# A fused attention and two feed-forward layers on one core: one bank pair used in halves, one conversion step less, other planned costs, and products of zeros in the first units

## The chip, the cores and the metric

The kernel runs on one core of a Trainium2 chip. The metric is device microseconds of one execution. The kernel before was run three times: median 749.57 us, from 743.37 to 752.7. One further execution was profiled; it took 745.85 us and its span, from the first to the last instruction, is 744.1 us.

## The reference, cut to what matters

```
scores = scale * q @ k.T ; causal mask ; a = softmax(scores) ; local = a @ v
q_p = phi(q)                                  # max(x, 0) + min(exp(x), 1)
mem_out = (q_p @ M_prev) / (q_p @ z_prev + 1e-6)
x = g * mem_out + (1 - g) * local             # g = sigmoid(beta), B=2 H=8 S=576 D=64
g1 = elu(x @ w_in) ; x = g1 @ w_out           # 1152 tokens, 512 -> 2048 -> 512
out = sum over 4 experts of p_e * (relu(x @ w1[e]) @ w2[e])   # 512 -> 1024 -> 512
```

All inputs are float32. The weights of the first feed-forward layer reach the kernel as 64-bit floats.

## The kernel before, in words

The work runs in two parts. In the first part the tokens are in two groups: 384 tokens (0 to 191 of both batches) and 768 tokens (the rest). Attention is cut into units, each a pair of heads: four units F0 to F3 for the first group (both batches at once), then eight units R00 to R13 for the second group. While the R units run, the first group goes through the first feed-forward layer (tiles ua, da; class Moe1) and the second one (ub, db; Moe2). The second part does both layers for the second group with a scheme of seven products for eight.

The order of the instructions is written by a planner (class Plan). Each step names its engine, a cost in us, a rank, the steps that it comes after, and the buffers that it takes and gives back. The planner keeps a clock for each engine and always starts the step with the lowest rank that can start at that time by those costs. So the costs (act_cost, dve_cost, pool_cost and the figures in the calls of add) set only the order on each engine; on the chip an engine runs its instructions in that order and waits on semaphores.

A unit does these steps: load, load_v (SyncE); split_h (ACT) and split_l (POOL, for F0 DVE) cut q and k into a high and a low part; phi_r, phi_e, phi_p (ACT) make phi(q); mem (PE, line 1226) multiplies phi(q) with the memory into a PSUM region om, and mem_a, mem_i, mem_f (DVE, 1202, 1240, 1208) divide it into tm; score (PE, 1273), lowest (DVE, 1287), exp (ACT, 1296), trans (PE, 1332), evac (1337 DVE, 1339 ACT), values (PE, 1346 and 1355) make the local part in a PSUM region ov, and sum_a, sum_i, sum_f (DVE) divide it into tv; both (POOL, 1386) adds tm to tv; turn (PE, 1392) transposes it, and join_h, join_l split it into xh and xl. Both regions om and ov lie in one tile o of two banks, of which there is one: SLOTS has "o": 1, mem takes it and sum_f gives it back, so the planner puts the next unit's mem behind this unit's sum_f.

Each of the 16 weight tiles that come as 64-bit floats is loaded in two halves of 512 KB (line 206), converted half by half, split into wh (ACT, 239) and wl (POOL, 243), and stored as 32-bit floats for the second part (keep, 235). A half's conversion is upper (ACT, 215), which scales the upper words into a bank, then on DVE shift (219), lower (223) and sign (229). All but the first tile wait in the plan for F3's last score (GATE). Each half has two buffers, given back by sign.

keep_busy puts products of zeros (line 297, one bank wide) ahead of a PE step for which the planner's clock showed a wait of over 0.3 us, until 140 us of that clock. Sixteen such products stand at the start.

Of the kernel before, what the change touches and what calls it, by code (L numbers as in the profile page):

```python
# [59 lines left out]
def tile_kernel(  # L60
# [53 lines left out]

    def plan_small(plan, rank):
# [12 lines left out]
        plan.add(("gate_e",), "act", 0.2, rank, gate_e, [("load_gate",)])  # L128
        plan.add(("gates",), "dve", 0.3, rank, gates, [("gate_e",)])
        plan.add(("probs",), "dve", 1.0, 30.0, setup_probs)  # L130

    def setup_probs():
        nc.sync.dma_start(out=pr, in_=probs)
# [19 lines left out]
    SLOTS = {  # L153
        "raw": 2, "rv": 2, "qh": 2, "ql": 2, "pe": 1, "pp": 2, "pt": 2, "nm": 4, "nr": 4, "tm": 1, "tv": 1,
        "ph": 4, "s0": 1, "s1": 1, "t": 1, "o": 1, "m": 3,
        "wr": 3, "w64_0": 2, "w64_1": 2, "w": NW, "h": 5, "ev": 3,
# [8 lines left out]
    }  # L165

    GATE = ("F3", "score20")
    UNIT1 = 5.0
# [14 lines left out]
    def plan_weights(plan, i, rank):  # L183
# [26 lines left out]
        def upper(half):  # L210
            if half == 0:
                block()
            _, high = t[half]
            t["cv", half] = abank("m" if i < W_EARLY else f"s{half}", f"cv{i}_{half}")
            nc.scalar.activation(out=t["cv", half], in_=high.bitcast(F32), func=AF.Copy, scale=2.0 ** -112)

# [4 lines left out]
        def lower(half):  # L221
            c, low = t["cv", half].bitcast(I32), t[half][0]
            nc.vector.scalar_tensor_tensor(  # L223
                out=c, in0=low, scalar=29, in1=c, op0=ALU.logical_shift_right, op1=ALU.bitwise_or
            )

        def sign(half):
            high, wi = t[half][1], t["wr"][:, 512 * half:512 * half + 512].bitcast(I32)
            nc.vector.scalar_tensor_tensor(
                out=wi, in0=high, scalar=-(2 ** 31), in1=t["cv", half].bitcast(I32),  # L230
                op0=ALU.bitwise_and, op1=ALU.bitwise_or,
            )
# [13 lines left out]
        if k < NW1 and not second:  # L246
            ends = []
            for half in range(2):
# [8 lines left out]
                add(f"shift{half}", "dve", dve_cost(512), lambda half=half: shift(half))  # L257
                add(f"lower{half}", "dve", dve_cost(512), lambda half=half: lower(half))
                ends.append(("w", i, f"sign{half}"))
                plan.add(  # L260
                    ends[-1], "dve", dve_cost(512), rank, lambda half=half: sign(half), [last[0]], [],
                    [f"w64_{half}", ("m", ("w", i, f"upper{half}")) if bank == "m" else bank],
# [25 lines left out]
    def attention_pools(stack):  # L288
# [4 lines left out]
        for name in ("s", "t", "o"):  # L293
            at[name] = pool("ps_" + name, bufs=1, space=PSUM)

    def nothing(ps):
        nc.tensor.matmul(
            ps.rearrange("p (n k) -> p n k", k=P), zeros, zeros.unsqueeze(1).to_broadcast([P, ps.shape[1] // P, P]),
            start=True, stop=True,
        )  # L300

    waits = [0]

    def keep_busy(ps):

        for _ in range(waits[0]):
            nothing(ps)
        waits[0] = 0
# [708 lines left out]
    def act_cost(n, psum=False):  # L1017
        return 0.833e-3 * n + (0.052 if psum else 0.093)

    def dve_cost(n, fast=False):  # L1020
        return (0.521e-3 if fast else 1.042e-3) * n + 0.069

    def pool_cost(n):
        return 2.1e-3 * n + 0.15

# [98 lines left out]
    def plan_unit(plan, kind, b, c, start, spare, slack):  # L1124
# [65 lines left out]
        if kind == "F":  # L1190
            add("phi_p", "act", act_cost(nq), phi_p, ["phi_e", "split_l"], gives=["raw"])
        else:
            add("phi_p", "pool", 2.5e-3 * nq + 0.2, phi_p, ["phi_e"])
            add("phi", "pool", pool_cost(nq), phi, ["phi_p", "split_l"], gives=["raw", "pe"])
# [11 lines left out]
        def times(ps, name, out):  # L1206
# [3 lines left out]
            )  # L1210

        def mem():
            o = at["o"].tile([P, 2, 512], F32, tag="o", name=f"o{uid}")
            keep_busy(o[:, 0])
            o = o[:, :, :2 * nt * DV].rearrange(
                "p a (w t d) -> p w a t d", w=2, d=DV
            )
            unit["om"], unit["ov"] = o[:, 0], o[:, 1]
            for t in range(nt):
                for bi, r0, r in parts_of(t):  # L1220
                    q = qcol[t] + 2 * r0
                    for odd in (0, 1):
                        rows = slice(D * odd, D * odd + D)
                        terms = ("e", "phi") if kind == "F" else ("phi",)
                        for x in terms:
                            nc.tensor.matmul(
                                unit["om"][r0:r0 + r, odd, t], unit[x][rows, q:q + r],
                                unit["rv"][rows, MEMORY[kind] + bi], start=x == terms[0], stop=x == terms[-1],
                            )

        def mem_f():
            unit["tm"] = atile([P, 3, 2, D], F32, tag="tm", name=f"tm{uid}")[:, :nt]
            times(unit["om"], "nm_", unit["tm"])

        if kind == "F":
            add("mem", "pe", 0.15 * 2 * nt, mem, ["phi_p", "load_v"], ["o"], ["pp", "pe"])
        else:
            add("mem", "pe", 0.15 * nt, mem, ["phi", "load_v"], ["o"], ["pp"])
        add("mem_a", "dve", 0.12, lambda: quotient(unit["om"], 1e-6, wmem, "nm_"), ["mem", ("gates",)], ["nr"])
        add("mem_i", "dve", 0.1, lambda: nc.vector.reciprocal(out=unit["nm_"], in_=unit["nm_"]), ["mem_a"])  # L1240
        add("mem_f", "dve", dve_cost(NQ), mem_f, ["mem_i"], ["tm"], ["nr"])


# [9 lines left out]
        def score(t, n):  # L1253
# [6 lines left out]
            for odd in (0, 1):  # L1260
                tag = "m" if "m" in s_from[t, n] else f"s{odd}"
                unit["s", odd, t, n] = abank(tag, f"s{uid}{odd}{t}{n}")
            keep_busy(unit["s", 0, t, n])
            for bi, r0, r in parts_of(t):
# [28 lines left out]
        def expo(odd, t):  # L1293
            k = 2 * t + len(segments(tiles[t][1])) - 1
            blk = row(odd, t)
            nc.scalar.activation(out=blk, in_=blk, func=AF.Exp, scale=-1.0, bias=unit["nm"][odd][:, k:k + 1])  # L1296

        for t, n, a, z_ in pieces:
            first, last = (t, n) == pieces[0][:2], (t, n) == pieces[-1][:2]
            add(  # L1300
                f"score{t}{n}", "pe", 3 * (z_ - a) / 2400 + 0.2, lambda t=t, n=n: score(t, n),
                ["split_l"] + ["score{}{}".format(*pieces[0])] * (not first), s_from[t, n] + ["pt", "nm", "nm"] * first, ["qh", "ql"] * last,
# [57 lines left out]
        for g, blks in enumerate(groups):  # L1360
            col, final = P * len(blks), g == len(groups) - 1
            add(
                f"trans{g}", "pe", 0.109 * len(blks), lambda g=g: transposes(g),
                sorted({f"exp{t}{odd}" for t, o, _ in blks for odd in ((0, 1) if o == 2 else (o,))})
# [8 lines left out]
            add(  # L1373
                f"values{g}", "pe", 0.115 * len(blks), lambda g=g: values(g),
                ["mem", f"evac{g}"] + [f"values{g - 1}"] * (g > 0), [], ["ph"] + ["rv", "nm", "nm"] * final,
            )
# [8 lines left out]
        def both():  # L1385
            nc.gpsimd.tensor_tensor(out=unit["tv"], in0=unit["tv"], in1=unit["tm"], op=ALU.add)

# [35 lines left out]
    with ExitStack() as first, tc.manual_schedule():  # L1423
# [8 lines left out]
        plan.awake, plan.last = IDLE_END, 0.43 * WARM - 0.5  # L1432
        plan_small(plan, OFFSET["load"] + 3.0)
        for c in range(H // 2):
# [107 lines left out]
```

## Time and profile before

| what | value |
|---|---|
| median of three runs | 749.57 us (743.37 to 752.7) |
| profiled execution | 745.85 us, span 744.1 us |
| PE busy | 729.4 us, 98% |
| DVE, ACT, POOL busy | 409.0, 355.4, 422.2 us |
| DMA, mean over the span | 108 GB/s |

PE is TensorE's matmul row, PEld its weight loads, SP the engine that issues the transfers. A busy PE is no PE at its peak: products of zeros and products at half the clock count as busy too. PEclk is the granted TensorE clock as a share of 2.4 GHz.

### The profile page before, as it was taken

Reading aid. Unit: us, or ns where it says so; the run is one execution under the profiler, and the core shown is the slowest. Engines: PE = TensorE matmul, PEld = TensorE weight load, DVE = VectorE, ACT = ScalarE, POOL = GpSimd, SP = SyncE. Lnnn points to the kernel's source line nnn. Section 1 sums busy time; section 2 is a strip of 40 time slices with the busy share of each in tenths; the row PEclk is TensorE's granted clock in tenths of the full one; section 3 lists DMA queues with packets and bytes.
Section 4 is the critical chain, followed back from the end, with each engine's and each line's share of the span. In section 5 each row is a group of like instructions: output and inputs, shape, how many; then the busy total and the mean of one; then the engine's idle time right before and its main releaser. Section 6 shows DMA issues by size and latency. Waiting matters only on the chain.

```text
span 744.1 us, 11247 instructions
## 1 busy us (share of the span) xinstructions
PE 729.4 (98%) x4339; PEld 651.2 (88%) x4339; DVE 409.0 (55%) x876; ACT 355.4 (48%) x609; POOL 422.2 (57%) x253
## 2 busy tenths in 40 slices
PE   8999989999999999999899999999999999999997
PEld 5688878898898898889799999998989989899896
DVE  3687897734524435423672774865636446364562
ACT  6648578665445444422585663753423224232230
POOL 4337676786365361436998747397666455664210
PEclk9989999999999999999999999999999999999999
DMA  7449698453332321313323231212303113031002
GB/s 237 127 138 351 227 300 297 153 164 124 101 112 80 106 86 50 102 43 110 100 62 109 85 102 41 64 51 85 92 26 111 57 57 96 22 110 57 1 0 85
DMA packets 23541, 80.38 MB, mean 108 GB/s; under 512 B 2880, under 2 KB 2880, under 8 KB 23488
## 3 DMA queue, kind: packets, MB, share of 16 engines
q1 hardware_dynamic: 23488, 79.66, 33.0%
q8 instruction: 34, 0.56, 0.3%
q14 instruction: 19, 0.16, 0.1%
HBM read 68.90 MB, written 10.75 MB: 107 GB/s over the span
## 4 chain that ended last, share of the span: by engine, by line
PE 86%; DVE 6%; ACT 3%; DMA 2%; POOL 2%; issue 1%; SPq 0%; DVEq 0%; ACTq 0%
PE db L273 9%; PE db L275 9%; PE db L274 9%; PE oR L1346 4%; PE da L275 4%; PE da L273 4%; PE da L274 4%; PE ub L273 3%; PE ub L275 3%; PE ub L274 3%; PE tR L1332 3%; PE sR L1273 2%; DVE cv L223 1%; DVE cv L219 1%; PE oR L1355 1%
## 5 line engine op out<-in xcount | busy, mean ns | idle before, releaser
L243 POOL TENSOR_TENSOR wl<-wr,wh 128x1024 fp32r<-128x1024 f32 x72 | 171.7, 2392 | 168.0 <-ACT wh L239 161.6
L239 ACT ACTIVATE wh<-wr 128x1024 fp32r<-128x1024 f32 x72 | 75.6, 1057 | 97.3 <-PE db L274 64.2
L273 PE MATMUL db<-wh,hb 128*128 128x512 f32 x288 | 115.1, 400 | 0.0
L275 PE MATMUL db<-wl,hb 128*128 128x512 f32 x288 | 112.8, 392 | 0.0
L274 PE MATMUL db<-wh,hb 128*128 128x512 f32 x288 | 112.6, 391 | 0.0
L987 DVE SCALAR_TENSOR_TENSOR acc<-db,pr,acc 128x512 f32<-128x512 f32 x42 | 31.5, 750 | 70.9 <-PE db L275 70.9
L275 PE MATMUL da<-ha,wh 128*128 128x384 f32 x192 | 65.9, 343 | 2.1 <-POOL ha L402 2.0
L273 PE MATMUL da<-ha,wh 128*128 128x384 f32 x192 | 66.4, 346 | 0.5 <-ACT ha L848 0.3
L274 PE MATMUL da<-ha,wl 128*128 128x384 f32 x192 | 65.2, 339 | 1.5 <-POOL wl L243 1.5
L273 PEld LDWEIGHTS db<-wh,hb 128*128 128x128 f32 x288 | 54.2, 188 | 11.9 <-issue 1.3
L275 PEld LDWEIGHTS db<-wl,hb 128*128 128x128 f32 x288 | 54.1, 188 | 11.7
L274 PEld LDWEIGHTS db<-wh,hb 128*128 128x128 f32 x288 | 54.2, 188 | 10.3
L502 DVE SCALAR_TENSOR_TENSOR hb<-ub,hb 128x384 fp32r<-128x384 f32 x32 | 17.7, 553 | 53.9 <-ACT hb L499 53.9
L273 PE MATMUL ub<-yh,wh 128*128 128x384 f32 x128 | 46.1, 360 | 0.0
L275 PE MATMUL ub<-yl,wh 128*128 128x384 f32 x128 | 43.1, 337 | 0.0
L274 PE MATMUL ub<-yh,wl 128*128 128x384 f32 x128 | 43.0, 336 | 0.0
L275 PEld LDWEIGHTS da<-ha,wh 128*128 128x128 f32 x192 | 36.6, 190 | 4.1 <-POOL ha L402 3.5
L273 PEld LDWEIGHTS da<-ha,wh 128*128 128x128 f32 x192 | 36.5, 190 | 2.1 <-issue 0.7
L274 PEld LDWEIGHTS da<-ha,wl 128*128 128x128 f32 x192 | 36.5, 190 | 2.1 <-POOL wl L243 2.1
L1296 ACT ACTIVATE ptR<-ptR,nmR 128x576 f32<-128x576 f32 (+2 forms) x48 | 30.3, 661 | 15.6 <-DVE nmR L1287 15.6
L1346 PE MATMUL oR<-rvR,pfR 128*128 128x65 f32 x288 | 37.5, 271 | 0.0
L1346 PEld LDWEIGHTS oR<-rvR,pfR 128*128 128x128 f32 x288 | 35.5, 192 | 1.0 <-issue 0.2
(883 smaller groups left out, 1869.2 us busy)
## 6 DMA issues: line engine op xcount, KB each, us to landing
wr<-in_w SPq DMA_DIRECT2D x64, 512.0 KB, 3.5
w<-in_w SPq DMA_DIRECT2D x32, 512.0 KB, 5.7
wscr<-wr SPq DMA_DIRECT2D x16, 512.0 KB, 6.7
wr<-wscr SPq DMA_DIRECT2D x16, 512.0 KB, 3.3
qkR<-in_qk_r SPq DMA_DIRECT2D x8, 480.0 KB, 5.8
rvR<-in_vm_r SPq DMA_DIRECT2D x8, 390.0 KB, 3.1
out<-acc SPq DMA_DIRECT2D x8, 256.0 KB, 2.0
qkF<-in_qk_f SPq DMA_DIRECT2D x4, 416.0 KB, 5.5
```

Of the source, the lines that this page charges most:

```text
L219: nc.vector.tensor_scalar(out=c, in0=c, scalar1=3, scalar2=None, op0=ALU.logical_shift_left)
L239: nc.scalar.activation(out=t["wh"], in_=t["wr"], func=AF.Copy)
L243: nc.gpsimd.tensor_tensor(out=wl, in0=t["wr"], in1=f32(t["wh"]), op=ALU.subtract)
L273: nc.tensor.matmul(out, ah, bh, start=first, stop=False)
L274: nc.tensor.matmul(out, al, bh, start=False, stop=False)
L275: nc.tensor.matmul(out, ah, bl, start=False, stop=last)
L502: nc.vector.scalar_tensor_tensor(out=t["h"][:, 1], in0=t["ps"], scalar=0.0, in1=f32(t["h"][:, 0]), op0=ALU.max, op1=ALU.subtract)
L987: nc.vector.scalar_tensor_tensor(out=acc, in0=t["ps"], scalar=p, in1=acc, op0=ALU.mult, op1=ALU.add)
L1273: nc.tensor.matmul(unit["s", odd, t, n][:, :w], unit[x][rows, q], unit[y][rows, ks[odd]], start=m == 0 and r0 == 0, stop=m == 2 and final,)
L1296: nc.scalar.activation(out=blk, in_=blk, func=AF.Exp, scale=-1.0, bias=unit["nm"][odd][:, k:k + 1])
L1332: nc.tensor.transpose(pst[:, P * n:P * n + P], src, ident)
L1346: nc.tensor.matmul(unit["ov"][:, odd, t], pf[:, col:col + P], unit["rv"][:, at_], start=j == 0, stop=False)
```

## The change

- The tile o becomes one tile sums, made once; om and ov are its left and right half (256 columns of each of the two banks) with a planner slot of their own ("om", "ov"). mem takes om, mem_f gives it back; the first values takes ov, sum_f gives it back. values no longer comes after mem. tm has two buffers.
- In F units phi_e and phi_p are added on POOL (step phi), as R units do, and mem multiplies the sum: one product for each pair of operands in place of two.
- F3 (hurried) leaves tm in PSUM and does its last addition on DVE in place of POOL.
- The conversion's sign step is gone: upper uses Prelu with a slope of 2^32 for negative words in place of Copy, and lower writes the result.
- F units put at least one product of zeros at the head of the first score and of each trans, and at least two of half the width at the head of mem and of the first values.
- The planned costs of ACT, DVE, POOL, score, mem, values and trans are other figures; the load of the probabilities is a step of its own with a later rank, and the gates have a later rank.
- The scratch for dynamic DMA is 1024 bytes.

```
-        "raw": 2, ... "tm": 1, "tv": 1,
-        "ph": 4, "s0": 1, "s1": 1, "t": 1, "o": 1, "m": 3,
+        "raw": 2, ... "tm": 2, "tv": 1,
+        "ph": 4, "s0": 1, "s1": 1, "t": 1, "om": 1, "ov": 1, "m": 3,
...
+    FEWEST = {"F": 1, "R": 0}
...
-        plan.add(("gate_e",), "act", 0.2, rank, gate_e, [("load_gate",)])
-        plan.add(("gates",), "dve", 0.3, rank, gates, [("gate_e",)])
-        plan.add(("probs",), "dve", 1.0, 30.0, setup_probs)
+        plan.add(("gate_e",), "act", 0.4, later, gate_e, [("load_gate",)])
+        plan.add(("gates",), "dve", 0.3, later, gates, [("gate_e",)])
+        plan.add(("load_probs",), "sync", 0.1, 20.0, load_probs)
+        plan.add(("probs",), "dve", 1.0, 30.0, setup_probs, [("load_probs",)])
...
-            nc.scalar.activation(out=t["cv", half], in_=high.bitcast(F32), func=AF.Copy, scale=2.0 ** -112)
+            nc.scalar.activation(
+                out=t["cv", half], in_=high.bitcast(F32), func=AF.Prelu, scale=2.0 ** -112, alpha=2.0 ** 32
+            )
...
         def lower(half):
-            c, low = t["cv", half].bitcast(I32), t[half][0]
+            low, wi = t[half][0], t["wr"][:, 512 * half:512 * half + 512].bitcast(I32)
             nc.vector.scalar_tensor_tensor(
-                out=c, in0=low, scalar=29, in1=c, op0=ALU.logical_shift_right, op1=ALU.bitwise_or
-            )
-
-        def sign(half):
-            high, wi = t[half][1], t["wr"][:, 512 * half:512 * half + 512].bitcast(I32)
-            nc.vector.scalar_tensor_tensor(
-                out=wi, in0=high, scalar=-(2 ** 31), in1=t["cv", half].bitcast(I32),
-                op0=ALU.bitwise_and, op1=ALU.bitwise_or,
+                out=wi, in0=low, scalar=29, in1=t["cv", half].bitcast(I32),
+                op0=ALU.logical_shift_right, op1=ALU.bitwise_or,
             )
...
+        at["sums"] = at["o"].tile([P, 2, 512], F32, tag="o", name="sums")
...
-    def keep_busy(ps):
+    def keep_busy(ps, least=0):
-        for _ in range(waits[0]):
+        for _ in range(max(waits[0], least)):
             nothing(ps)
...
     def act_cost(n, psum=False):
-        return 0.833e-3 * n + (0.052 if psum else 0.093)
-    def dve_cost(n, fast=False):
-        return (0.521e-3 if fast else 1.042e-3) * n + 0.069
+        return 0.833e-3 * n + (0.09 if psum else 0.13)
+    def dve_cost(n):
+        return 1.042e-3 * n + 0.115
     def pool_cost(n):
-        return 2.1e-3 * n + 0.15
+        return 2.1e-3 * n + 0.2
...
         if kind == "F":
             add("phi_p", "act", act_cost(nq), phi_p, ["phi_e", "split_l"], gives=["raw"])
+            add("phi", "pool", pool_cost(nq), phi, ["phi_p"], gives=["pe"])
...
+        def side(what):
+            keep_busy(at["sums"][:, 0, 256 * what:256 * what + 256], 2 * FEWEST[kind])
+            return at["sums"][:, :, 256 * what:256 * what + nt * DV].rearrange("p a (t d) -> p a t d", d=DV)
...
-                        terms = ("e", "phi") if kind == "F" else ("phi",)
-                        for x in terms:
-                            nc.tensor.matmul(
-                                unit["om"][r0:r0 + r, odd, t], unit[x][rows, q:q + r],
-                                unit["rv"][rows, MEMORY[kind] + bi], start=x == terms[0], stop=x == terms[-1],
-                            )
+                        nc.tensor.matmul(
+                            unit["om"][r0:r0 + r, odd, t], unit["phi"][rows, q:q + r],
+                            unit["rv"][rows, MEMORY[kind] + bi], start=True, stop=True,
+                        )
+        hurried = uid == f"F{H // 2 - 1}"
...
-        if kind == "F":
-            add("mem", "pe", 0.15 * 2 * nt, mem, ["phi_p", "load_v"], ["o"], ["pp", "pe"])
-        else:
-            add("mem", "pe", 0.15 * nt, mem, ["phi", "load_v"], ["o"], ["pp"])
+        mem_cost = 0.2 + 0.224 * sum(len(parts_of(t)) for t in range(nt))
+        add("mem", "pe", mem_cost, mem, ["phi", "load_v"], ["om"], ["pp"])
...
-            keep_busy(unit["s", 0, t, n])
+            keep_busy(unit["s", 0, t, n], FEWEST[kind] * (n == t == 0))
...
-            keep_busy(pst)
+            keep_busy(pst, FEWEST[kind])
...
         def values(g):
+            if g == 0:
+                unit["ov"] = side(1)
...
-                ["mem", f"evac{g}"] + [f"values{g - 1}"] * (g > 0), [], ["ph"] + ["rv", "nm", "nm"] * final,
+                [f"evac{g}", "load_v"] + [f"values{g - 1}"] * (g > 0), ["ov"] * (g == 0), ["ph"] + ["rv", "nm", "nm"] * final,
...
-        add("sum_f", "dve", dve_cost(NQ), sum_f, ["sum_i"], ["tv"], ["o", "nr"])
-        add("both", "pool", pool_cost(NQ), both, ["sum_f", "mem_f"], gives=["tm"])
+        add("sum_f", "dve", dve_cost(NQ), sum_f, ["sum_i"], ["tv"], ["ov", "nr"])
+        eng = ("dve", dve_cost(NQ)) if hurried else ("pool", pool_cost(NQ))
+        add("both", *eng, both, ["sum_f", "mem_f"], gives=["om" if hurried else "tm"])
```

## Rows read from the trace of the kernel before

**Rows 1.** The page: busy time, share of the span and instructions of each engine.

```profile
PE 729.4 (98%) x4339; PEld 651.2 (88%) x4339; DVE 409.0 (55%) x876; ACT 355.4 (48%) x609; POOL 422.2 (57%) x253
```

**Rows 2.** Windows by stage: start:end, length, busy us of each engine, clock, DMA share, GB/s.

```profile
6.40:48.20 41.80, 39.71 (x405) 29.50 (x405) 25.44 (x95) 24.86 (x54) 12.33 (x9) 0.92 0.47 151
...
56.70:66.20 9.50, 7.68 (x32) 6.13 (x32) 8.89 (x15) 7.15 (x14) 7.72 (x5) 0.83 0.98 329
66.20:126.00 59.80, 56.33 (x325) 50.71 (x324) 47.97 (x88) 42.98 (x76) 41.44 (x26) 1.00 0.85 300
...
140.00:300.00 160.00, 160.00 (x1083) 138.56 (x1082) 69.12 (x191) 76.42 (x121) 86.35 (x48) 1.00 0.34 110
300.00:400.00 100.00, 97.60 (x553) 87.07 (x553) 45.74 (x91) 49.29 (x85) 65.79 (x39) 0.98 0.29 92
```

**Rows 3.** Windows of the products of zeros alone (line 297), PE's busy time first.

```profile
6.40:48.20 41.80, 11.23 (x45) 0.92 0.47 151
...
56.70:66.20 9.50, 1.78 (x10) 0.96 (x10) 0.83 0.98 329
66.20:126.00 59.80, 4.04 (x19) 1.61 (x19) 1.00 0.85 300
```

**Rows 4.** Windows of 1 us, PE: busy time, granted clock, DMA share, GB/s.

```profile
35.00:36.00 1.00, 1.00 (x16) 0.80 0.22 90
36.00:37.00 1.00, 0.56 (x4) 0.50 0.00 0
...
42.00:43.00 1.00, 1.00 (x11) 0.79 0.00 0
```

**Rows 5.** The chain that ended last, 20 to 50 us: start, us, what.

```profile
20.85 0.38 PE oF L1346 x2
...
21.31 0.56 DVE tmF L1208
...
25.98 1.50 PE oF L1226 x32
```

**Rows 6.** Timeline of PE: start, us, instructions, and in brackets what ended an idle.

```profile
36.49 1.03 PE L297 MATMUL oF<-zeros 128*128 128x512 bf16 x2 [0.44 <-DVE tvF L1208]
...
44.48 2.12 PE L297 MATMUL xF<-zeros 128*128 128x512 bf16 x9
```

**Rows 7.** Timelines of DVE and POOL in the first units.

```profile
19.74 0.19 DVE L1240 RECIPROCAL nm_F<-nm_F 128x6 f32<-128x6 f32 x1
...
45.77 1.00 POOL L1386 TENSOR_TENSOR tvF<-tvF,tmF 128x384 f32<-128x384 f32 x1 [8.17 <-DVE tvF L1208]
```

**Rows 8.** Single lines over the whole span: duration in ns min/median/max.

```profile
L229 DVE SCALAR_TENSOR_TENSOR wr<-w,cv x32: 675/687/689, 26.5 to 131.8; 128x512 int32<-128x512 int32 x32
...
L215 ACT ACTIVATE cv<-w x32: 606/630/658, 18.5 to 129.7; 128x512 f32<-128x512 f32 x32
...
L1181 POOL TENSOR_TENSOR ppR<-peR,ppR x8: 992/1016/1026, 77.8 to 264.2; 128x384 f32<-128x384 f32 x8
...
L1158 ACT ACT_TABLE_LOAD  x1: 1283/1283/1283, 0.7 to 0.7; - x1
```

**Rows 9.** The chain that ended last, 48 to 75 us.

```profile
55.58 0.70 DVE wr L229
...
57.44 2.40 POOL wl L243
...
62.87 0.69 PE da L275
```

**Rows 10.** Timeline of POOL: the first and the last of seven wl in this stretch.

```profile
83.79 2.40 POOL L243 TENSOR_TENSOR wl<-wr,wh 128x1024 fp32r<-128x1024 f32 x1 [1.50 <-ACT wh L239]
...
114.42 2.40 POOL L243 TENSOR_TENSOR wl<-wr,wh 128x1024 fp32r<-128x1024 f32 x1 [3.06 <-issue]
```

**Rows 11.** The DMA queue's waits; a window with its DMA share and GB/s last.

```profile
SPq L206 <- DVE wr L229: 68.7, 27, 12.8
...
72.00:76.00 4.00, 4.00 (x26) 3.59 (x25) 0.65 (x4) 2.01 (x4) 4.00 (x3) 1.00 1.02 371
```

More of the change, by code (lines that the diff above doesn't have):

```diff
@@ L113, in tile_kernel, with plan_small @@
     prs = const.tile([P, 9], F32, name="prs")
-    def plan_small(plan, rank):
+    def plan_small(plan, rank, later):
         def load_gate():
@@ L127, in plan_small, with load_probs @@
         plan.add(("load_gate",), "sync", 0.1, rank, load_gate)
-        plan.add(("gate_e",), "act", 0.2, rank, gate_e, [("load_gate",)])
-        plan.add(("gates",), "dve", 0.3, rank, gates, [("gate_e",)])
-        plan.add(("probs",), "dve", 1.0, 30.0, setup_probs)
+        plan.add(("gate_e",), "act", 0.4, later, gate_e, [("load_gate",)])
+        plan.add(("gates",), "dve", 0.3, later, gates, [("gate_e",)])
+        plan.add(("load_probs",), "sync", 0.1, 20.0, load_probs)
+        plan.add(("probs",), "dve", 1.0, 30.0, setup_probs, [("load_probs",)])
+    def load_probs():
+        nc.sync.dma_start(out=pr, in_=probs)
     def setup_probs():
-        nc.sync.dma_start(out=pr, in_=probs)
         nc.vector.reduce_sum(out=prs, in_=pr, axis=mybir.AxisListType.X)
@@ L153, in tile_kernel @@
     SLOTS = {
-        "raw": 2, "rv": 2, "qh": 2, "ql": 2, "pe": 1, "pp": 2, "pt": 2, "nm": 4, "nr": 4, "tm": 1, "tv": 1,
-        "ph": 4, "s0": 1, "s1": 1, "t": 1, "o": 1, "m": 3,
+        "raw": 2, "rv": 2, "qh": 2, "ql": 2, "pe": 1, "pp": 2, "pt": 2, "nm": 4, "nr": 4, "tm": 2, "tv": 1,
+        "ph": 4, "s0": 1, "s1": 1, "t": 1, "om": 1, "ov": 1, "m": 3,
         "wr": 3, "w64_0": 2, "w64_1": 2, "w": NW, "h": 5, "ev": 3,
@@ L257, in plan_weights @@
                 add(f"shift{half}", "dve", dve_cost(512), lambda half=half: shift(half))
-                add(f"lower{half}", "dve", dve_cost(512), lambda half=half: lower(half))
-                ends.append(("w", i, f"sign{half}"))
+                ends.append(("w", i, f"lower{half}"))
                 plan.add(
-                    ends[-1], "dve", dve_cost(512), rank, lambda half=half: sign(half), [last[0]], [],
+                    ends[-1], "dve", dve_cost(512), rank, lambda half=half: lower(half), [last[0]], [],
                     [f"w64_{half}", ("m", ("w", i, f"upper{half}")) if bank == "m" else bank],
@@ L1017, in act_cost, with values_cost @@
     def act_cost(n, psum=False):
-        return 0.833e-3 * n + (0.052 if psum else 0.093)
-    def dve_cost(n, fast=False):
-        return (0.521e-3 if fast else 1.042e-3) * n + 0.069
+        return 0.833e-3 * n + (0.09 if psum else 0.13)
+    def dve_cost(n):
+        return 1.042e-3 * n + 0.115
     def pool_cost(n):
-        return 2.1e-3 * n + 0.15
+        return 2.1e-3 * n + 0.2
+    def values_cost(blocks):
+        return sum(0.224 if odd < 2 else 0.45 for _, odd, _ in blocks)
     class Plan:
@@ L1210, in times @@
             )
+        def side(what):
+            keep_busy(at["sums"][:, 0, 256 * what:256 * what + 256], 2 * FEWEST[kind])
+            return at["sums"][:, :, 256 * what:256 * what + nt * DV].rearrange("p a (t d) -> p a t d", d=DV)
         def mem():
[L1213 to L1216, printed above, removed]
-            )
-            unit["om"], unit["ov"] = o[:, 0], o[:, 1]
+            unit["om"] = side(0)
             for t in range(nt):
@@ L1223, in mem @@
                         rows = slice(D * odd, D * odd + D)
-                        terms = ("e", "phi") if kind == "F" else ("phi",)
-                        for x in terms:
-                            nc.tensor.matmul(
-                                unit["om"][r0:r0 + r, odd, t], unit[x][rows, q:q + r],
-                                unit["rv"][rows, MEMORY[kind] + bi], start=x == terms[0], stop=x == terms[-1],
-                            )
+                        nc.tensor.matmul(
[3 more added lines that the diff above has]
+        hurried = uid == f"F{H // 2 - 1}"
         def mem_f():
+            if hurried:
+                unit["tm"] = unit["om"][:, :, :, :D].rearrange("p a t d -> p t a d")
+                times(unit["om"], "nm_", unit["tm"])
+                return
             unit["tm"] = atile([P, 3, 2, D], F32, tag="tm", name=f"tm{uid}")[:, :nt]
             times(unit["om"], "nm_", unit["tm"])
-        if kind == "F":
-            add("mem", "pe", 0.15 * 2 * nt, mem, ["phi_p", "load_v"], ["o"], ["pp", "pe"])
-        else:
-            add("mem", "pe", 0.15 * nt, mem, ["phi", "load_v"], ["o"], ["pp"])
+        mem_cost = 0.2 + 0.224 * sum(len(parts_of(t)) for t in range(nt))
+        add("mem", "pe", mem_cost, mem, ["phi", "load_v"], ["om"], ["pp"])
         add("mem_a", "dve", 0.12, lambda: quotient(unit["om"], 1e-6, wmem, "nm_"), ["mem", ("gates",)], ["nr"])
         add("mem_i", "dve", 0.1, lambda: nc.vector.reciprocal(out=unit["nm_"], in_=unit["nm_"]), ["mem_a"])
-        add("mem_f", "dve", dve_cost(NQ), mem_f, ["mem_i"], ["tm"], ["nr"])
+        add("mem_f", "dve", dve_cost(NQ), mem_f, ["mem_i"], [] if hurried else ["tm"], ["nr"] if hurried else ["nr", "om"])
         pieces = [(t, n, a, z_) for t in range(nt) for n, (a, z_) in enumerate(segments(tiles[t][1]))]
@@ L1296, in expo, with score_cost @@
             nc.scalar.activation(out=blk, in_=blk, func=AF.Exp, scale=-1.0, bias=unit["nm"][odd][:, k:k + 1])
+        def score_cost(t, w):
+            return len(parts_of(t)) * max(3 * w / 2400, 0.32) + 0.24
         for t, n, a, z_ in pieces:
@@ L1300, in plan_unit @@
             add(
-                f"score{t}{n}", "pe", 3 * (z_ - a) / 2400 + 0.2, lambda t=t, n=n: score(t, n),
+                f"score{t}{n}", "pe", score_cost(t, z_ - a), lambda t=t, n=n: score(t, n),
                 ["split_l"] + ["score{}{}".format(*pieces[0])] * (not first), s_from[t, n] + ["pt", "nm", "nm"] * first, ["qh", "ql"] * last,
@@ L1362, in plan_unit @@
             add(
-                f"trans{g}", "pe", 0.109 * len(blks), lambda g=g: transposes(g),
+                f"trans{g}", "pe", 0.109 * len(blks) + 0.06, lambda g=g: transposes(g),
                 sorted({f"exp{t}{odd}" for t, o, _ in blks for odd in ((0, 1) if o == 2 else (o,))})
@@ L1373, in plan_unit @@
             add(
-                f"values{g}", "pe", 0.115 * len(blks), lambda g=g: values(g),
-                ["mem", f"evac{g}"] + [f"values{g - 1}"] * (g > 0), [], ["ph"] + ["rv", "nm", "nm"] * final,
+                f"values{g}", "pe", values_cost(blks), lambda g=g: values(g),
+                [f"evac{g}", "load_v"] + [f"values{g - 1}"] * (g > 0), ["ov"] * (g == 0), ["ph"] + ["rv", "nm", "nm"] * final,
             )
@@ L1385, in both @@
         def both():
-            nc.gpsimd.tensor_tensor(out=unit["tv"], in0=unit["tv"], in1=unit["tm"], op=ALU.add)
+            eng = nc.vector if hurried else nc.gpsimd
+            eng.tensor_tensor(out=unit["tv"], in0=unit["tv"], in1=unit["tm"], op=ALU.add)
         def turn():
@@ L1432, in tile_kernel @@
         plan.awake, plan.last = IDLE_END, 0.43 * WARM - 0.5
-        plan_small(plan, OFFSET["load"] + 3.0)
+        plan_small(plan, OFFSET["load"] + 3.0, 1.5)
         for c in range(H // 2):
@@ L1531 @@
     }
-    nc = bacc.Bacc("TRN2", target_bir_lowering=False, num_devices=1)
+    nc = bacc.Bacc("TRN2", target_bir_lowering=False, num_devices=1, dynamic_dma_scratch_size=1024)
     args = [
```

## The prediction

> **What bounds the kernel now.** The page comes first: PE is busy for 98% of the span and no other engine for more than 57% [rows 1]. So only what PE spends on nothing can be won back, and that has to be found by stage. The windows by stage [rows 2] show where: from 140 to 300 us PE is busy in every microsecond at the full clock, 2.4 GHz, and from 300 to 400 it lacks 2.4 us. Nothing in the change touches that second stretch, so I book nothing after 140 us. What is left lies in three stages.
>
> *First units, 6.4 to 48.2 us (41.8 us).* PE is idle for 41.8 - 39.7 = 2.1 us [rows 2]. Products of zeros take 11.2 us of its busy time, 45 of them [rows 3]. The granted clock falls to the lower level, 1.2 GHz, from 36 to 42 us (six rows of 0.50, with 0.80 and 0.79 on either side) [rows 4]; in the microseconds before it PE was busy throughout, with small products. That loses 0.2 + 6 x 0.5 + 0.2 = 3.4 us, of which some 0.7 fall on an idle and on zeros that are counted already: 2.7. Real work at the full clock is thus 41.8 - 2.1 - 11.2 - 2.7 = 25.8 us. The stage is bound by dependences between engines, not by PE's work.
>
> *The first feed-forward products, 56.7 to 66.2 us (9.5 us).* 1.8 us idle, 1.8 us of zeros, and a clock of 0.83, which loses 0.17 x 9.5 = 1.6 us [rows 2, 3]: about 5 us.
>
> *The conversions, 66.2 to 126 us.* 3.5 us idle and 4.0 us of zeros: 7.5 us at most. DVE is busy for 48.0 of 59.8 us here and the DMA engines at a share of 0.85 [rows 2].
>
> So 14 to 16 us in the first stage and 12.5 us in the next two bound any gain, if everything were perfect.
>
> **The change part by part.** *mem with the sum of phi.* One unit's mem took 1.50 us for 32 records [rows 5]; half of them go: 0.75 x 4 units = 3.0 us off PE. In return POOL adds for each F unit; the R units' addition takes 1.016 us for 384 columns [rows 8], 1.19 us for 448 by columns, 4.7 us for four units. POOL is busy for 12.3 of 41.8 us [rows 2], and F3's last addition (1.00 us, [rows 7]) leaves it, so the addition itself is hidden. What can show is its place in POOL's queue: a split_l of the next unit ahead of it would keep mem, and all of PE behind mem, waiting.
>
> *Halves.* F3's mem began behind F2's sum_f: 0.44 us of idle and two products of zeros of 1.03 us, at the half clock [rows 6]. With a slot of its own mem can go earlier, so up to 1.5 us here. But the two regions stay in the same two banks. The trace shows what that means: F1's tmF reads om and its factors were ready when the reciprocal ended at 19.93 us [rows 7], yet it started only at 21.31, when the products of line 1346, which write ov, had ended [rows 5]. DVE stood for 1.4 us. Readers of one half and writers of the other thus take turns in the order of issue, and the planner, before as after, does not know it. With mem and values of neighbouring units free to be mixed there are more such turns. From nothing (all reads done before PE comes) to one read of 0.56 us [rows 5] for each of 12 writes (mem and two values groups in four units), 6.7 us; I take 1.5, near the one case seen.
>
> *Zeros at least.* Seven products for each F unit: four of 256 columns, three of 512. Nine of 512 took 2.12 us [rows 6], with the last one's end about 0.22 apiece; 0.11 for half the width is an estimate by columns. 4 x 0.11 + 3 x 0.22 = 1.1 us, 4.4 us in four units. Where PE would wait they are free, as most of the 45 are now; I take half, 2.2 us. On the other side they stand just where the clock fell. If it stays up, 2.7 us come back; as the fall came with no idle ahead of it, more products are nearer to a cure than fewer, and I take it whole.
>
> *F3's end.* DVE adds in place of POOL: one DVE pass of this size is 0.56 us [rows 5] against 1.00 [rows 7], and it is needed before the first feed-forward product: 0.5 us.
>
> *Loads and gates.* One small transfer and two small ACT steps leave the start; PE's first sixteen products of zeros last until 6.4 us anyway. Nothing, up to 0.5 us.
>
> First stage: 3.0 + 1.5 + 2.7 + 0.5 - 1.5 - 2.2 = 4.0 us. Its ends: 9 us (no turns, zeros all covered, and some idle gone), and a loss of 6.7 + 4.4 - 3.0 = 8 us.
>
> *Conversion.* 32 DVE instructions of 0.687 us go [rows 8], 22 us of DVE in all. Prelu in place of Copy is one ACT instruction of the same shape, 0.630 us [rows 8]; that its slope costs nothing is taken from the shape alone. In the second stage the chain runs through DVE to wr (55.58), then POOL's wl at 57.44, then the ha behind it on POOL, then PE at 62.87 [rows 9]. Six sign steps (two for each of tiles 1 to 3, the last at 55.58) lie on DVE ahead of it, 6 x 0.69 = 4.1 us; without them wl would start by 53.3. What is late next is ha itself: its own chain from the last ua, through ACT, DVE and POOL, ends some 3 us after ua whatever the weights do. So of 5 us about 3 come back; ends 0 and 5.
>
> In the third stage seven tiles came at (114.42 - 83.79) / 6 = 5.1 us each [rows 10]. DVE gives each of them six steps, 4.1 us, and other work the rest; with four, 2.7 us, DVE is no longer what the loads wait for (68.7 us in total now [rows 11]). Next is the transfer: 1.57 MB for each tile (1.05 in, 0.52 out), 4.2 us at the 371 GB/s of a full window [rows 11], 5.2 us at the mean of 300 [rows 2]. I take the middle, 4.7: 0.4 x 7 = 2.8 us sooner, and book 3; ends 0 and 6.
>
> *Planned costs.* They move no work, only the order. That can win or lose a microsecond anywhere; it is in the ends.
>
> **Sum.** Against the profiled execution: 745.85 - 4 - 3 - 3 = 735.9 us. That execution lies 3.7 us under the median of the three runs (749.57), so I put the forecast half of that higher: 737 us. The runs spread over 9 us; 2%, 15 us, is about what a measurement of this kernel can tell from no change.
>
> **The rivals.** *Transfers pace the weights.* The share of 0.98 and 0.85 [rows 2] speaks for it, the 68.7 us of waits on DVE [rows 11] against it. Then the second and third term go: 745.85 - 4 = 742.
>
> *All of it comes back.* 9 + 5 + 6 = 20 us: 726. For it: each loss has a named cause that the change touches. Against: it needs the turns to cost nothing and the transfers to run at their best.
>
> *Turns on the banks (slower).* PE meets a read that is not done at each of the 12 writes, with nothing else to do as it runs in order: 8 us lost, as worked out. The eight R units add their mem in a stage where PE has no idle at all: 8 x 0.56 = 4.5 us at most, of which I take half. As the conversions wait for F3's last score, the weights come later too and the other two terms are gone: 745.85 + 8 + 2 = 756. It decides as soon as DVE, by the plan ahead of PE, is on the chip behind it. Against it: of all such pairs before, PE waited for a sum's read only once, 0.44 us [rows 6].
>
> *Prelu needs another table.* The profile has one table load, of 1.283 us, for Exp, Copy and Relu together [rows 8]. Were Prelu elsewhere, each conversion between two Exps would cost two loads: 32 x 2 x 1.283 = 82 us on ACT between 18.5 and 130 us, where it has 17 + 2 + 17 = 36 us free in the three stages [rows 2]; some 46 us longer, 792. The Trainium skill (ScalarE: Activation LUTs, Table sets) says that functions of different sets cost a load at each change and that cheap functions come with every set; it does not name Prelu among its examples. By the second half of that rule nothing is added, by the first half the rival holds; the single load in the trace agrees with both.
>
> **How the numbers follow.** Forecast 0.50, transfers 0.21, all of it 0.14, turns 0.11, table 0.04. The range leaves out the table, the upper half of the turns and the far end of "all of it": 723 to 754. Faster by over 2%: all of it and the best end of the forecast, 0.20. Slower by over 2%: the table and the worst of the turns, 0.06. Within 2%: 0.74.
>
> **What would show it.** Right: the first ua product 3 to 6 us sooner than 48.2 and no row at 0.50 before it; DVE's conversions at four steps a tile and wl at under 5 us; PE busy throughout from 66 on. Wrong: PE waiting for tmF or tvF, or DVE for PE writes to the other half (turns); PE waiting for POOL's phi; wl still at 5.1 us with a DMA share near 1 (transfers); more than one table load. The prediction fails most easily in the first stage, since a new order there can put any wait in the place of the old ones.

## The result and the profile after

The changed kernel took 735.53 us (median; 734.19 to 736.48) beside 746.91 us for the kernel before: a ratio of 0.985, 95% interval 0.980 to 0.990, 11 us less. Its profiled execution took 736.48 us with a span of 734.7 us, where the sum of the prediction had 735.9.

The page's line of busy time:

```profile
PE 722.6 (98%) x4263; PEld 647.8 (88%) x4263; DVE 391.9 (53%) x845; ACT 352.9 (48%) x609; POOL 425.8 (58%) x256
```

It says little: PE stands at 98% as before [rows 1], DVE has 17 us less and POOL 4 us more. The windows by stage, the first two cut at about the same work as before, the later ones ending at the same times (columns as in [rows 2]):

```profile
6.40:43.60 37.20, 35.55 (x341) 26.72 (x340) 26.01 (x97) 25.02 (x56) 18.03 (x12) 0.91 0.55 181
52.10:61.00 8.90, 8.10 (x45) 6.87 (x44) 5.93 (x10) 5.89 (x10) 6.77 (x6) 1.00 0.98 334
61.00:126.00 65.00, 62.58 (x406) 57.38 (x404) 46.82 (x101) 50.23 (x88) 48.76 (x30) 1.00 0.86 306
140.00:300.00 160.00, 159.99 (x1047) 136.42 (x1048) 67.54 (x186) 71.31 (x113) 81.29 (x44) 1.00 0.31 100
```

and the products of zeros in the first three of them (line 300 now):

```profile
6.40:43.60 37.20, 12.43 (x45) 3.94 (x44) 0.91 0.55 181
52.10:61.00 8.90, 1.48 (x8) 0.71 (x8) 1.00 0.98 334
61.00:126.00 65.00, 0.82 (x4) 0.31 (x4) 1.00 0.86 306
```

The first units end 4.6 us sooner with as many products of zeros as before, 45, and as low a mean clock. Around the first da products the loss is 0.8 us idle and 1.5 us of zeros at the full clock, 2.3 us where it was about 5 [rows 2, 3]. From there to 126 us it is 2.4 + 0.8 = 3.2 us, where it was 7.5. These windows end at 126 us whatever work is left by then, so the losses are not what was won; the points below are the measure.

Two rows, from the products by tile, give two of three points that all kernels of this study share: the first product of the first layer (ua, 43.6 us) and the first of the second part (pa10A, 352.2 us), with the end of the span as the third (durations in ns, then first and last start in us):

```profile
L274 PE MATMUL ua<-xh,wh x64: 332/334/470, 43.6 to 124.4; 128*128 128x384 f32 x64
...
L274 PE MATMUL pa10A<-xB11h,wh48A x4: 333/334/334, 352.2 to 354.8; 128*128 128x384 f32 x4
```

Before, these points lay at 48.2 and 361.6 us. So 4.6 us were won up to ua, 313.4 - 308.6 = 4.8 us from ua to the second part, and nothing behind that (382.5 us in both). The same three stretches for every kernel, from one profiled execution each:

| kernel | that execution, us | first ua | ua to second part | second part to end |
|---|---|---|---|---|
| before | 745.85 | 48.2 | 313.4 | 382.5 |
| changed | 736.48 | 43.6 | 308.6 | 382.5 |
| changed, run again | 735.46 | 42.4 | 308.8 | 382.4 |
| conversion alone | 742.56 | 51.6 | 306.9 | 382.3 |
| changed, old conversion | 740.90 | 42.9 | 313.7 | 382.5 |
| changed, no least zeros | 731.51 | 40.1 | 307.2 | 382.4 |
| changed, om given back late | 732.66 | 41.9 | 306.5 | 382.5 |
| planned costs alone | 747.01 | 50.7 | 312.0 | 382.5 |
| changed, mem in two terms | 738.90 | 47.8 | 306.8 | 382.4 |
| changed, three times the zeros | 740.75 | 48.5 | 307.9 | 382.5 |
| late om, gates' load first | 734.45 | 43.0 | 307.2 | 382.5 |
| changed, one conversion step | 729.62 | 39.3 | 306.1 | 382.4 |
| changed, F3 not hurried | 741.76 | 45.0 | 312.5 | 382.5 |

The changed kernel's two executions differ by 1.2 us at ua with the same instructions, so a difference under some 1.5 us in that column means nothing. In the next column the kernels that have the new conversion with two steps and differ only in what the F units do range from 306.5 to 308.8, without the last row of the table, so a difference of 2 us there means little either. The last experiment on the zeros (c12) has no row here and is told without its profiled execution, which fell in a slow state (789.85 us at a mean clock of 0.839).

### The profile page after: what moved, and what is told of

Same layout as the page of the kernel before. It is cut to its first block, busy times and chain, and to the rows that moved or that the text cites. A ratio compares the mean times of both kernels' runs of the same rounds, so it can differ in the third digit from the quotient of the medians.

```text
span 734.7 us, 11055 instructions
## 1 busy us (share of the span) xinstructions
PE 722.6 (98%) x4263; PEld 647.8 (88%) x4263; DVE 391.9 (53%) x845; ACT 352.9 (48%) x609; POOL 425.8 (58%) x256
## 4 chain that ended last, share of the span: by engine, by line
PE 88%; DMA 4%; ACT 3%; DVE 2%; POOL 1%; issue 1%; SPq 0%; DVEq 0%; ACTq 0%
PE db L274 9%; PE db L276 9%; PE db L275 9%; PE sums L1361 5%; PE da L274 4%; PE da L276 4%; PE da L275 4%; PE ub L274 4%; DMA w<-in_w 3%; PE ub L276 3%; PE ub L275 3%; PE sR L1283 2%; PE tR L1345 2%; PE sums L1370 2%; PE sums L1231 1%; DMA wmem<-in_beta 1%
## 5 line engine op out<-in xcount | busy, mean ns | idle before, releaser
L990 DVE SCALAR_TENSOR_TENSOR acc<-db,pr,acc 128x512 f32<-128x512 f32 x42 | 31.5, 751 | 70.0 <-PE db L276 69.2
L274 PE MATMUL da<-ha,wh 128*128 128x384 f32 x192 | 65.7, 342 | 0.0
L276 PE MATMUL da<-ha,wh 128*128 128x384 f32 x192 | 64.6, 336 | 0.8 <-POOL ha L405 0.8
L1352 ACT ACTIVATE pfR<-tR 128x512 f32<-128x512 f32 x24 | 14.3, 594 | 49.3 <-PE tR L1345 49.3
L1361 PE MATMUL sums<-rvR,pfR 128*128 128x65 f32 x288 | 37.5, 271 | 0.0
L533 DVE SCALAR_TENSOR_TENSOR acc<-db,pr,acc 128x512 f32<-128x512 f32 x21 | 15.8, 751 | 40.4 <-PE db L276 40.1
L502 ACT ACTIVATE hb<-ub 128x384 fp32r<-128x384 f32 x32 | 15.7, 491 | 43.7 <-PE ub L276 43.7
L1361 PEld LDWEIGHTS sums<-rvR,pfR 128*128 128x128 f32 x288 | 35.3, 191 | 1.2 <-DVE tmR L1216 0.2
```

The source lines that it names most:

```text
L274: nc.tensor.matmul(out, ah, bh, start=first, stop=False)
L276: nc.tensor.matmul(out, ah, bl, start=False, stop=last)
L502: nc.scalar.activation(out=t["h"][:, 0], in_=t["ps"], func=AF.Relu)
L533: nc.vector.scalar_tensor_tensor(out=acc, in0=t["ps"], scalar=p, in1=acc, op0=ALU.mult, op1=ALU.add)
L990: nc.vector.scalar_tensor_tensor(out=acc, in0=t["ps"], scalar=p, in1=acc, op0=ALU.mult, op1=ALU.add)
L1361: nc.tensor.matmul(unit["ov"][:, odd, t], pf[:, col:col + P], unit["rv"][:, at_], start=j == 0, stop=False)
```

## The experiments

**The conversion, alone and undone.** c1_conv_alone is the kernel before with

```
-   upper: func=AF.Copy, scale=2.0 ** -112 ; shift ; lower -> cv ; sign -> wr
+   upper: func=AF.Prelu, scale=2.0 ** -112, alpha=2.0 ** 32 ; shift ; lower -> wr
```

and c2_no_conv is the changed kernel with these lines turned back.

> The kernel before with the two-step conversion alone. If the conversion carries the later half of the gain, as the prediction has it (3 + 3 us, less what of the first stage is its own): 4 to 7 us under the kernel before, first ua product still near 48 us, wl tiles under 5 us apart. If the transfers pace the weights: within 1.5 us of before, wl tiles still 5.1 us apart. If one chain carries all of it (conversion is all that counts): 9 to 11 us under.

> The changed kernel with the three-step conversion back. If the parts add: 4 to 7 us over the changed kernel, ua still first at 43.5 to 44.5 us, the loss in the stretch from there to 126 us. If the transfers pace the weights: no more than 1.5 us over the changed kernel. If the earlier start of the first stage is only handed on to a wait for weights: ua early, but 9 us over the changed kernel, at the time of the kernel before.

Measured: c1 0.994 of before (0.991 to 0.998), c2 0.996 (0.994 to 0.999), 743.6 us against 735.5 for the changed kernel, 8 us longer. That is near the least that was expected of c1, and a microsecond over the most that was expected of c2. c2's profiled execution, 740.9 us, is one of the two shortest of its ten (to 745.0), so the table shows only part of its loss; no trace shows the rest. In the table the stretch from ua to the second part falls into two classes: 312.0 to 313.7 with the old conversion, 306.5 to 308.8 with the new one in two steps, with one exception that is taken up below. The conversion is worth 5.1 us there with everything else changed and 6.5 us with nothing else. That transfers alone pace the old conversion falls.

c1 shows something that neither theory expected: ua comes 3.4 us later than before. The longest wait of PE in it, and POOL's timeline at that place:

```profile
PE xF L1388 <- POOL tvF L1382: 3.5, 1, 3.5
```

```profile
45.84 2.35 POOL L240 TENSOR_TENSOR wl<-wr,wh 128x1024 fp32r<-128x1024 f32 x1 [6.74 <-ACT wh L236]
48.16 1.00 POOL L1382 TENSOR_TENSOR tvF<-tvF,tmF 128x384 f32<-128x384 f32 x1
```

The weight tile that is now ready sooner stands ahead of F3's last addition in POOL's queue, 2.35 us of it, behind a wait for ACT. Before, the addition ran at 45.77 [rows 7], ahead of that tile. The wait costs more than its 3.5 us: behind it the granted clock stands at 0.50 from 49 to 55 us, on both sides of the first ua product.

**F3's end.** c11_not_hurried:

```
-   hurried = uid == f"F{H // 2 - 1}"
+   hurried = False
```

> The changed kernel with F3 like the other F units: tm in SBUF and the last addition on POOL. The prediction books 0.5 us for it. If so: ua 0.3 to 0.7 us later and the whole 0 to 1 us longer, hardly to be told. Rival: the last unit's chain is the path to ua, with POOL's 1.0 us and one more hand-over on it: 1 us or more.

Measured: 740.13 us, ratio 0.991 (0.988 to 0.995): 4.6 us longer than the changed kernel, the rival's case. POOL's timeline in it:

```profile
40.58 2.37 POOL L245 TENSOR_TENSOR wl<-wr,wh 128x1024 fp32r<-128x1024 f32 x1 [7.58 <-ACT wh L241]
42.92 0.99 POOL L1402 TENSOR_TENSOR tvF<-tvF,tmF 128x384 f32<-128x384 f32 x1
```

Again wl runs first, and PE's transpose waits 1.5 us for tvF behind ten products of zeros. In the changed kernel this addition is DVE's. So a part of the change that reads like a saving of 0.5 us takes away the collision that the faster conversion makes. Not all of the 4.6 us is explained by it: only 1.4 to 2.6 us of it lie ahead of ua. The addition began 1.6 us after tvF was ready at 41.32, and POOL takes 0.44 us longer for it than DVE. Behind ua this is the exception in the table, 312.5 us with the new conversion. Its stretch from the first da (54.5) to 126 us has 3.6 us of zeros and a mean clock of 0.98, where the changed kernel has 1.1 us and 1.00; that is another order of all steps from there on, and which of them brings it was not tried.

**mem.** c6_two_terms:

```
-   add("phi", "pool", ...) ; matmul(om, phi, rv, start=True, stop=True)
+   for x in ("e", "phi"): matmul(om, x, rv, start=x == "e", stop=x == "phi")   # F units
```

> The changed kernel with mem in F units as two products for each pair of operands again and without POOL's addition. If the 3.0 us that the prediction books for mem are all on the path: ua about 3 us later than 43.6, the rest as in the changed kernel. If PE's work is no bound in this stage, since it is paced by dependences: less than 1 us. If POOL's addition costs more than the halved mem saves: ua sooner.

Measured: 739.81 us, ratio 0.990 (0.987 to 0.993), 4.6 us over the changed kernel beside it; ua at 47.8, 4.2 to 5.4 us later, so all of the loss lies ahead of it. The chain's row for one unit's mem in the changed kernel says what is saved directly:

```profile
24.51 0.87 PE sums L1231 x16
```

1.50 us [rows 5] less 0.87 is 0.63 us, 2.5 us for four units. Most of the rest is a turn on the two banks, the mechanism of the prediction's slower rival. DVE's rows for F3's mem_f, which works in om, and PE's for the second group of values, which write ov:

```profile
40.93 0.57 DVE L1215 TENSOR_TENSOR sums<-sums,nm_F 128x384 f32<-128x384 f32 x1 [1.72 <-PE sums L1362]
```

```profile
42.47 0.43 PE L1362 MATMUL sums<-rvF,pfF 128*128 128x65 f32 x2 [1.58 <-DVE pfF L1351]
```

DVE stands for 1.72 us until PE has written the other half, its copy of pfF comes behind that, and PE waits 1.58 us for the copy. The changed kernel's order does not meet this; c6's does.

**Halves.** c4_slot_back leaves the two halves but gives om back only behind sum_f, so that the plan holds the next mem back as before:

```
-   mem_f gives ["nr", "om"] ; sum_f gives ["ov", "nr"]
+   mem_f gives ["nr"]       ; sum_f gives ["ov", "nr", "om"]     # not for F3, where "both" gives om
```

> The changed kernel with om given back only by sum_f, so that the planner puts the next mem behind this unit's sum_f as before. If the slot of its own is worth what the prediction took (1.5 us less 1.5 us of turns): within 1 us of the changed kernel, since F3's mem waits for tvF on the chip either way. Rival (halves carry the first stage): ua 3 us later or more.

Measured: 732.82 us (732.16 to 734.89), ratio 0.982 (0.978 to 0.987); ua 0.5 to 1.7 us sooner than in the changed kernel. That is 2.4 to 2.7 us under the changed kernel, where at most 1 us either way was expected. The slot of its own is worth nothing, and the plan without it is if anything the better one. In the changed kernel's timeline F3's mem waits where it did before [rows 6]:

```profile
32.42 0.58 PE L300 MATMUL sums<-zeros 128*128 128x256 bf16 x2 [0.66 <-DVE tvF L1216]
```

tvF there reads F2's ov, the other half: the slot was free, the banks were not. c4 has the same row with 0.67 us. Both halves are also one tile of the program; whether the bank or the tile makes them take turns was not tried.

**Zeros at least.** c3_no_zeros and c8_more_zeros change one figure:

```
-   FEWEST = {"F": 1, "R": 0}
+   FEWEST = {"F": 0, "R": 0}      # c3;  {"F": 3, "R": 0} in c8
```

> The changed kernel without the least number of zero products (the planner's own stay). The prediction's step was that half of them are hidden (2.2 us shown) and that they keep the clock up (2.7 us). In the changed kernel the clock fell all the same from 32.4 to 39 us, so I now expect the zeros to be a cost: ua 1 to 2.5 us sooner than 43.6. Rival: without them the clock falls sooner or longer, rows of 0.50 well before 32 us, and ua comes at 45 us or later.

> The changed kernel with three in place of one (and six in place of two) zero products at the least at these heads, 13.2 us of them in place of 4.4. If zeros are a cost wherever they are forced (taking them out moved ua from 43.6 to 40.1): ua 5 to 9 us later. If they keep the clock up when there are enough: no row at 0.50 between 6.4 us and ua, 3 us won back, and ua no more than 5 us later.

Measured: c3 736.79 us, ratio 0.986 (0.980 to 0.992); c8 742.31 us, ratio 0.994 (0.991 to 0.997). c3's profiled execution is the fastest of its four: ua at 40.1 us, 731.51 us, mean clock 0.995. The other three took 735.91 to 738.51 us at 0.991 to 0.983. Judged by its trace, taking the zeros out wins 5 us; judged by its runs, it wins nothing. In c8's profiled execution the granted clock is 1.00 for the whole of the first units:

```profile
6.40:48.50 42.10, 41.05 (x398) 1.00 0.49 162
```

but ua comes 5 to 6 us later. The clock did not fall there, at a price above what its fall costs in the changed kernel. c10 below kept it as well, with no more than the changed kernel's least zeros.

c12_slot_no_zeros joins c3 and c4, to see whether c3's spread was chance.

> om given back by sum_f and no least number of zero products. Without the zeros alone one profiled execution took 731.5 us and three others 736 to 738.5, at mean clocks from 0.995 down to 0.983; with them the spread was 2 us. If the forced zeros buy a steady clock: executions spread over 5 us or more here, from about 728 to 737, at clocks that go with them. If the spread was chance: 728 to 731 throughout.

Measured: ratio 0.987 (0.982 to 0.992), executions from 735.21 to 739.70 us at mean clocks of 0.988 to 0.975. With the zeros and the same plan of slots, c4 and c9 took 732.16 to 734.89 us at 0.987 to 0.997. So no execution of c12 came down to the longest of c4 and c9: with this plan of slots the least zeros win some 3 us, although the one trace of c3 seems to say the opposite. The lower mean clocks point to the clock as the reason; where in c12 it fell, no trace of these executions shows.

**Planned costs alone.** c5_costs_alone:

```
-   act 0.052/0.093, dve 0.069, pool 0.15      # fixed parts, us
+   act 0.09/0.13,   dve 0.115, pool 0.2
```

> The kernel before with the new figures in act_cost, dve_cost and pool_cost and nothing else: no work is moved, only the order. By the prediction: within 2 us of before (order only, either way). Rival: the better figures carry the gain of the first stage; then ua comes 4 us sooner than 48.2 and the whole is 4 us or more under before.

Measured: 748.91 us, ratio 1.003 (1.000 to 1.006): no gain, and ua 2.5 us later. Figures nearer to the durations in the trace did not by themselves give a better order. The new figures for score, mem, values and trans were left out of this run, and no run takes any of the new figures out of the changed kernel, so what they do in it is not shown.

**The changed kernel again.**

> The changed kernel itself on this chip, as the measure for the three beside it: 735 to 738 us, ua first at about 43.6 us, 308.6 us from there to the first product of the second part and 382.5 us from that to the end.

Measured: 735.20 us, ratio 0.983 (0.980 to 0.985); ua at 42.4.

**What limits the weights now.** c10_one_step leaves the shift out as well:

```
-   add(f"shift{half}", "dve", dve_cost(512), lambda half=half: shift(half))
```

> The changed kernel with the conversion's shift left out as well (the weights of the first layer are then wrong numbers), one DVE step for each half. Going from three steps to two won 5 us between the first ua product and the second part. If transfers pace the weights now, as the prediction has it as the next limit: within 1 us of the changed kernel. If DVE still paces them: 3 to 5 us under it. If PE is fed well enough already, with some 3 us idle or on zeros left: 0.5 to 3 us under.

Measured: 730.80 us, ratio 0.979 (0.975 to 0.983), 4.4 to 4.7 us under the changed kernel. 2.5 us of it lie between ua and the second part, the rest ahead of ua, where the clock stayed at 1.00 in the profiled execution. The time is that of the case "DVE still paces them", but the trace does not bear that case out. c4, which has both steps, is as short between ua and the second part (306.5 us against 306.1), and over 66 to 126 us PE is fed as well in c4 (first row) as in c10 (second):

```profile
66.00:126.00 60.00, 59.66 (x392) 54.27 (x391) 45.53 (x101) 47.56 (x82) 46.03 (x30) 1.00 0.82 286
```

```profile
66.00:126.00 60.00, 59.74 (x411) 53.55 (x410) 34.18 (x83) 49.01 (x83) 43.45 (x27) 1.00 0.80 276
```

DVE has 11 us less to do there, and PE is hardly busier for it. The eighth and the fourteenth wl start at 69.47 and 102.64 us, 5.5 us a tile, where the changed kernel has 4.84; from the second to the sixteenth it is 5.1 against 5.4. So the stretch fits the third case, PE fed well enough already, and whether transfers come next is left open.

**The gates' load first.** c9_gates_first is c4 with

```
-   plan_small(plan, OFFSET["load"] + 3.0, 1.5)
+   plan_small(plan, OFFSET["load"] - 1.0, 1.5)
```

> The kernel with om given back by sum_f (732.8 us), and the load of the gates' vector as the first transfer, since in the changed kernel its landing at 7.4 us held DVE and then PE (0.8 us idle and 0.7 us of zeros). If the first unit's wait is on the path: 1 to 1.5 us under 732.8. If a later wait in the first units absorbs it: 732 to 733.5. Rival: the first q and k land 0.4 us later and the sixteen opening products no longer cover it: 733.5 or more.

Measured: 733.13 us, ratio 0.981 (0.978 to 0.985). The time is the same as c4's: the second case by the number. But the wait that it was to remove was not there: in c4 PE waits only 0.2 us at that place, and so it does in the changed kernel's second profiled execution, where the vector's first use begins at 6.24 us and not at 7.46. The 0.8 us were one execution's, and what such a wait costs was not tried. Of the kernels that leave no work out, c4 and c9 are the fastest, by some 2 us under the changed one, hardly outside the spread.

## Why the prediction held, point by point

**The sum.** 737 us against 735.5; against the profiled execution 735.9 against 736.5. (Half of 3.7 on top of 735.9 would be 737.7.) The three stages: 4.0 booked and 4.6 measured up to ua; 3 + 3 booked and 4.8 measured from there to 140 us and on; nothing booked and nothing measured behind. The stages were right, and what moved each was partly right. The R units use the halves and run beyond 140 us too, and PE is still busy for 159.99 of 160 us from there to 300, so the loss that the turns rival gave them did not come. PE is not busy throughout from 66 us on, as it was to be: it lacks 1.3 us up to 140.

**First units.** The terms inside the 4.0 were mis-sized and made up for each other; that their sum came within 0.6 us is luck.
- mem was booked at 3.0; it is 2.5 by its own durations, and undoing it costs 4.6, with the turn that its order then meets.
- Halves were booked at 1.5 less 1.5 of turns: nothing, which c4 bears out, or less than nothing. The turn that PE was to take on the other half's read is there, once, 0.66 us.
- The clock was booked as cured, 2.7 us. This step failed. The changed kernel's clock, in windows of 1 us:

```profile
33.00:34.00 1.00, 1.00 (x12) 0.50 0.00 0
...
38.00:39.00 1.00, 1.00 (x7) 0.50 0.81 324
```

  It stands at 1.2 GHz for six microseconds as before [rows 4], around the same step, F3's mem, and this time with PE's 0.66 us of idle ahead of it. So by these rows none of the 2.7 us came back in this execution; in the other profiled one the clock takes 1.7 us in place of 3.4. The least zeros go with a higher mean clock over several executions (c12 beside c4 and c9), which one profile before and one after can't show.
- The zeros' own price was booked at 2.2 us. Against c3's trace it is 2.3 to 3.5 us; the 2.3 is against the execution of the changed kernel that lost as much to the clock as c3 did, 1.7 us by windows of 1 us, so the term was well sized. With the clock counted over several executions the zeros win.
- F3's end was booked at 0.5; undoing it costs 4.6, of which 1.4 to 2.6 us lie in this stage. What was not seen is that the conversion's own success puts wl ahead of that addition on POOL.
- The gates' load was booked at nothing. Its landing at 7.4 us did hold DVE, and PE for 0.8 us, in one of two executions; no run tells what that cost.
- With the clock at nothing, the terms as the runs size them (mem 2.5, F3's end 1.4 to 2.6, zeros -2.3) make 1.6 to 2.8 us of the 4.6. Where the rest comes from was not split; the order that the planned costs make is the part that no run took back.

**First da products.** 3 of 5 us were booked, and 2.7 us of the loss are gone. wl and ha on POOL are sooner, as the chain of [rows 9] said, and ha is late next: PE's waits there are 0.8 us on ha alone.

**Conversions.** The eighth and the fourteenth wl tile, those of [rows 10], now start at

```profile
75.95 2.42 POOL L245 TENSOR_TENSOR wl<-wr,wh 128x1024 fp32r<-128x1024 f32 x1
...
104.98 2.37 POOL L245 TENSOR_TENSOR wl<-wr,wh 128x1024 fp32r<-128x1024 f32 x1 [1.70 <-issue]
```

7.8 and 9.4 us sooner, at (104.98 - 75.95) / 6 = 4.84 us each, where 4.7 was taken. The reason given for 4.7, that transfers come next, is neither shown nor ruled out: with one DVE step less still, the same tiles of c10 are 5.5 us apart. The DMA queue still waits 57.4 us for DVE's wr (68.7 before [rows 11]).

**Prelu.** The new instruction and the table loads of the changed kernel:

```profile
L221 ACT ACTIVATE cv<-w x32: 604/622/647, 17.2 to 111.8; 128x512 f32<-128x512 f32 x32
```

```profile
L1165 ACT ACT_TABLE_LOAD  x1: 1283/1283/1283, 0.7 to 0.7; - x1
```

0.622 us against 0.630 for Copy [rows 8], and one load in the whole span: the table rival is out. The Trainium skill (ScalarE: Activation LUTs, Table sets) says that cheap functions come with every set; by this trace Prelu is one that comes with Exp's.

**POOL's addition of phi** is nowhere among PE's waits; it was hidden, as booked.

**Planned costs** were booked at nothing of their own with a microsecond either way; c5 gives +0.3% (0.0 to 0.6) for three of the figures in the kernel before; in the changed kernel they stand untested.

## What to carry to other kernels

When a step is made shorter, look at what its result triggers and whose queue that enters: the faster conversion alone sent a 2.4 us weight step ahead of the 1.0 us addition for which PE was waiting, and cost 3.4 us at that place before it won 6.5 behind it. In a kernel whose PE is at 98%, cut the span at points that all variants share and sum by stage; here the last stretch stayed within 382.3 to 382.5 us in all thirteen executions, so that each difference could be placed. Before a faster variant is taken as proof of a limit, see whether its gain lies in the stretch where that limit was meant to be, and whether another variant without the step gets there too. Judge anything that acts on the clock by several executions, not by the profiled one.

## What was not expected of the hardware

With the same instructions the granted clock's falls come at other moments and for other lengths: 6 us at half the clock in one execution of the changed kernel and ua at 43.6, a shorter fall and ua at 42.4 in another, of which these are two rows:

```profile
34.00:35.00 1.00, 1.00 (x5) 0.50 0.00 0
...
37.00:38.00 1.00, 1.00 (x12) 0.95 0.82 274
```

Without the least zeros the mean clock of the executions compared (c3 and c12) ranged from 0.995 to 0.975 and the time by 8 us; with them (the changed kernel, run twice, c4 and c9), from 0.997 to 0.987 and by 4 us. The clock is not all of a spread: c8's twelve executions lie at 0.991 to 0.998 and still 7 us apart.
